# Loads in rows of 8 KB instead of 2, one load tied to another product, and another written-out order for the first block of a fused retention and two-layer feed-forward kernel

## The chip, the cores and the metric

The kernel runs on one core of one Trainium2 chip. The metric is device time in microseconds (us) of one execution, lower is better. Times before the change are a median of 3 runs.

## The reference

Retention (attention with a decaying mask and no softmax) over 4 sequences of 576 positions with 8 heads of 64, then two feed-forward layers over all 2304 tokens, 512 wide inside and 2048 wide in the middle. Everything is float32.

```
scores = scale * q @ k.T                      # per batch and head
ret    = scores * D,  D[i, j] = gamma_h ** (i - j) for i >= j, else 0
x      = (ret @ v) as tokens x 512
x      = leaky(x @ w_in)  @ w_out             # leaky(h) = max(0.01 h, h), weights moe
out    = (h * cos(h)) @ w_out2, h = x @ w_in2 # weights moe2
```

## The kernel before

Every float32 product of the two layers is made of three float32r products: each operand is split into a high part and the low rest, and low*high, high*low and high*high are added up in PSUM. Retention uses plain float32 products of 64 by 64.

Tokens go in 18 chunks of 128 (chunk i) and in 5 blocks (512, 512, 512, 384, 384 tokens). Block 0 is chunks 0 to 3. The middle of 2048 is 16 groups of 128 (f = 0 to 15). A weight group comes from HBM as one tile `raw` of 1 MB (128 partitions of 8 KB) that holds w_in and w_out of that group; the kernel must undo an encoding of the 64-bit words on ScalarE and VectorE and split the result before TensorE can use it. Group 0 and group 15 come as two halves, a (w_in) and b (w_out).

What runs until the end of block 0 is an order written out by hand, the string `FIRST`; each word is a step, and on each engine the instructions stand in the order of the words. The words, with i a chunk and f a group:

- `chI` loads a chunk's q, k, k, v (1 MB, SyncE's queue; chunk 0 in two loads, q and k first); `sqI`, `svI` scale q (VectorE, L249) and v (VectorE L261, or eight small operations on ScalarE, L256).
- `sI` scores (TensorE, L297), `mI` their mask (VectorE, L318), `vI` scores times values (L335), `gI` growth, k times v (L359), `stI.0`, `stI.1` the running state (VectorE, L381 and L383), `rI.0`, `rI` the products with the state (L398), `tkI` copies the result to `xr` (ScalarE, L437). `VI` does v and r of chunk I and g and s of chunk I + 1 in one go.
- `rawF` loads a weight group (L468; halves L473), `absF` and `loF` are ScalarE's part of decoding it (L486, L490), `csF` (two operations, L494 and L496), `orF` (L503) and `addF` (L510) VectorE's; `hiF` is the high part (ScalarE, L519), `lowF` the low rest (VectorE, L522).
- `xhP`, `xlP` split block 0's input (ScalarE L534, VectorE L538; four parts). `HF.P` is the first product of group F (12 products of 512 columns, L550), `lkF`, `ghF`, `glF` leaky and the split of its result (ScalarE L575, L580, VectorE L585), `OF` the second product (12 products, L564).
- `~N` is N times 128 columns of products with a tile of zeros, whose result nobody reads (L456). Of the four such words in the list before all four emit products, 3 + 4 + 5 + 13.

After the list a planner orders blocks 1 to 4, the second layer (products L1197 and L1369) and the conversion of its weights; it works from fixed durations and is the same for any list. The second layer's weights come in pieces of 256 KB, loaded by `convert` (L1052).

All loads are issued by SyncE in the list's order. A wait of one load holds back all loads behind it. Two kinds of such waits are put in by hand with `in_turn`: `raw1` and `raw0b` wait for the scores of chunk 1, and `ch4`, `raw2`, `raw3` wait for the last growth product issued before them (chunk 3's).

The host lays the arrays out. Before, qkv is kept as [chunk][4][128][512], so that one partition's part of a chunk is four pieces of 2 KB, and w as [layer][group][4][128][256 words], also pieces of 2 KB; the loads gather them with a rearranged view.

Of the kernel before, what the change touches and what calls it, by code (L numbers as in the profile page):

```python
# [50 lines left out]


FIRST = """
ch0 sq0 s0 sv0 m0 raw0a abs0a cs0a or0a ~3 v0 g0 st0.0 st0.1 ~4 r0.0 ch1 sq1 s1 r0 lo0a add0a ch2 m1 sq2 sv1
hi0a low0a v1 g1 s2 st1.0 st1.1 r1.0 sv2 m2 v2 r1 ch3 sq3 sv3 raw0b raw1 tk0 g2 st2.0 st2.1 s3 m3 abs0b tk1
cs0b or0b lo0b add0b r2.0 r2 v3 g3 st3.0 st3.1 ~5 r3.0 r3 abs1 cs1 or1 lo1 hi0b low0b add1 tk2 tk3 xh0 xl0 xh1
xl1 ch4 sq4 xh2 xl2 xh3 xl3 hi1 low1 raw2 raw3 abs2 cs2 ~13 H0.0 H0.1 H0.2 H0.3 H1.0 H1.1 H1.2 H1.3 lk0 gh0
gl0 lo2 abs3 or2 add2 lk1 gh1 O0 gl1 O1 cs3 hi2 low2 H2.0 H2.1 H2.2 H2.3 sv4 V3 raw4 lo3 or3 add3 abs4 cs4 hi3
low3 raw5 raw7 raw6 raw8 ch5 raw9 raw15a or4 lk2 gh2 gl2 lo4 add4 abs5 cs5 H3.0 H3.1 H3.2 H3.3 O2 hi4 lk3 low4
H4.0 H4.1 H4.2 H4.3 gh3 gl3 O3 lo5 or5 add5 abs6 cs6 hi5 lk4 gh4 low5 H5.0 H5.1 H5.2 H5.3 gl4 O4 lo7 lo6 abs7  # L60
or6 add6 cs7 hi6 low6 lk5 gh5 gl5 or7 add7 H6.0 H6.1 H6.2 H6.3 O5 abs8 cs8 hi7 lk6 low7 H7.0 H7.1 H7.2 gh6 gl6
st4.0 or8 lo8 add8 st4.1 raw10 lo10 sq5 raw11 H7.3 lk7 gh7 gl7 m4 O6 O7 hi8 low8 H8.0 H8.1 abs9 abs10 lo9 sv5
cs9 or9 add9 raw12 cs10 hi9 low9 H8.2 H8.3 V4 ch6 or10 lk8 gh8 st5.0 gl8 st5.1 add10 abs11 cs11 H9.0 H9.1 H9.2
H9.3 lk9 gh9 gl9 O8 O9 or11 tk4 hi10 low10 H10.0 H10.1 H10.2 H10.3 raw15b raw13 lo11 add11 raw14 sv6 sq6 m5 V5
ch7 abs12 hi11 lk10 gh10 cs12 low11 gl10 or12 lo12 add12 lo13 abs13 H11.0 H11.1 H11.2 H11.3 lk11 gh11 hi12 sv7
lo14 cs13 gl11 st6.0 m6 st6.1 sq7 O10 O11 tk5 low12 H12.0 or13 add13 hi13 H12.1 H12.2 H12.3 lk12 gh12 abs14
low13 abs15a gl12 V6 st7.0 st7.1 cs14 or14 H13.0 H13.1 H13.2 H13.3 add14 lk13 gh13 gl13 O12 O13 cs15a hi14
low14 or15a abs15b tk6 lo15b cs15b ch8 H14.0 H14.1 H14.2 H14.3 sq8 sv8 lo15a m7 add15a hi15a low15a V7 st8.0
lk14 gh14 gl14 st8.1 tk7 H15.0 H15.1 H15.2 H15.3 O14 lk15 or15b add15b gh15 gl15 hi15b low15b O15 m8 ch9 sq9
sv9  # L70
"""


# [1468 lines left out]
```

## Time and profile before

| | |
|---|---|
| median of 3 runs | 834.29 us (833.98 to 834.76) |
| the profiled execution | 833.8 us, of which its span 831.7 us |
| TensorE (PE) busy | 810.5 us, 97% of the span |
| VectorE (DVE) busy | 647.2 us, 78% |
| ScalarE (ACT) busy | 543.8 us, 65% |
| mean granted TensorE clock | 0.994 of full speed |
| DMA | 203.78 MB, mean 245 GB/s |

The span runs from the first to the last instruction; 2.1 us of the execution lie around it. Busy time of PE counts a product until its modelled end, so a busy PE is not PE at its peak. "PEld" is PE's load of the stationary operand, which overlaps its products. All times below are us from the span's start.

### The profile page before, as it was taken

How to read it: one execution, taken by the hardware profiler on the slowest of the kernel's cores; microseconds unless marked ns; L12 is line 12 of the kernel's file. 1: busy time of each engine (PE TensorE's matmuls, PEld its weight loads, DVE VectorE, ACT ScalarE, POOL GpSimd, SP SyncE). 2: the span in 40 equal slices, each digit the busy share in tenths (PEclk: the TensorE clock that was granted, in tenths of full speed). 3: DMA queues.
4: the chain of work that ended last, by engine and by line, in shares of the span. 5: the costliest groups of instructions: out<-in, count | busy, mean ns of one | idle time of the engine just before them, and what ended most of it. 6: DMA issues, size and time to landing. Idle time of an engine off the chain costs nothing.

```text
span 831.7 us, 16073 instructions
## 1 busy us (share of the span) xinstructions
PE 810.5 (97%) x6134; PEld 742.4 (89%) x6134; DVE 647.2 (78%) x1148; ACT 543.8 (65%) x1041; POOL 5.8 (1%) x8
## 2 busy tenths in 40 slices
PE   6999999999999999999999999999999999999996
PEld 4678887888888889999999989989999999999986
DVE  5899987888887868678731297898896888977994
ACT  4788866555555546457432598876878876688761
POOL 0000011000000000000000000000000000000000
PEclk9999999999999999999999999999999999999999
DMA  8774626887777787767688599797866587565632
GB/s 320 271 263 152 229 54 203 267 251 231 266 252 251 244 264 243 250 208 229 216 279 353 209 325 347 239 382 273 290 241 247 218 336 271 169 262 193 250 143 110
DMA packets 101308, 203.78 MB, mean 245 GB/s; under 512 B 9072, under 2 KB 54896, under 8 KB 96112
## 3 DMA queue, kind: packets, MB, share of 16 engines
q1 hardware_dynamic: 101088, 202.41, 69.6%
q8 instruction: 48, 0.79, 0.4%
q10 hardware_dynamic: 144, 0.35, 0.2%
q14 instruction: 28, 0.23, 0.1%
HBM read 147.42 MB, written 55.31 MB: 244 GB/s over the span
## 4 chain that ended last, share of the span: by engine, by line
PE 81%; DVE 8%; DMA 4%; issue 3%; ACT 3%; SPq 0%; DVEq 0%; POOLq 0%; ACTq 0%
PE psum L564 20%; PE psum L550 20%; PE psum L1369 19%; PE psum L1197 19%; DMA ch<-in_qkv 1%; DMA raw<-in_w 1%; PE psum L335 1%; DVE w L522 1%; PE psum L359 1%; DMA ws<-ws 1%; PE psum L398 1%; DVE t L510 1%; DVE t L503 1%; DVE g L1268 1%; PE psum L297 1%
## 5 line engine op out<-in xcount | busy, mean ns | idle before, releaser
L550 PE MATMUL psum<-x_sb,w 128*128 128x512 f32 (+1 forms) x960 | 212.1, 370 | 0.8 <-DVE x_sb L538 0.6
L564 PE MATMUL psum<-g,w 128*128 128x512 f32 (+1 forms) x960 | 211.6, 370 | 0.1
L550 PEld LDWEIGHTS psum<-x_sb,w 128*128 128x128 f32 x960 | 174.7, 188 | 26.1 <-DVE x_sb L538 1.3
L564 PEld LDWEIGHTS psum<-g,w 128*128 128x128 f32 x960 | 174.3, 188 | 24.9 <-DVE g L585 1.6
L1197 PE MATMUL psum<-x,ws 128*128 128x384 f32 x576 | 112.2, 335 | 2.5 <-DMA ws<-ws 1.4
L1197 PEld LDWEIGHTS psum<-x,ws 128*128 128x128 f32 x576 | 100.7, 188 | 3.8 <-DMA ws<-ws 1.7
L1369 PE MATMUL psum<-g,wp 128*128 128x384 f32 x432 | 85.1, 340 | 5.0 <-ACT g L1272 2.8
L851 DVE TENSOR_TENSOR g<-graw,g 128x512 fp32r<-128x512 f32 (+1 forms) x64 | 39.9, 623 | 60.0 <-ACT g L848 59.4
L1197 PE MATMUL psum<-x,wa 128*128 128x384 f32 x432 | 85.2, 335 | 0.0
L1369 PEld LDWEIGHTS psum<-g,wp 128*128 128x128 f32 x432 | 76.3, 190 | 7.2 <-ACT g L1272 3.5
L1369 PE MATMUL psum<-g,wq 128*128 128x384 f32 x432 | 82.3, 334 | 0.1
L1197 PEld LDWEIGHTS psum<-x,wa 128*128 128x128 f32 x432 | 75.8, 188 | 0.2 <-DVE h L1227 0.2
L1369 PEld LDWEIGHTS psum<-g,wq 128*128 128x128 f32 x432 | 75.5, 188 | 0.4 <-DVE acc L1406 0.4
L848 ACT CAST g<-graw 128x512 fp32r<-128x512 f32 (+1 forms) x64 | 36.3, 567 | 52.6 <-PE psum L564 52.4
L844 ACT ACTIVATE graw<-psum 128x512 f32<-128x512 f32 (+1 forms) x64 | 34.6, 541 | 52.5 <-PE psum L550 52.4
L1406 DVE TENSOR_TENSOR acc<-psum,acc 128x384 f32<-128x384 f32 x90 | 49.7, 554 | 18.4 <-PE psum L1369 18.1
L1255 DVE SCALAR_TENSOR_TENSOR h<-r,h 128x768 f32<-128x768 f32 x48 | 45.7, 952 | 15.2 <-ACT r L1252 15.1
L1268 DVE TENSOR_TENSOR g<-tq,g 128x768 fp32r<-128x768 f32 x48 | 45.6, 953 | 6.6 <-ACT g L1272 6.0
L1246 DVE SCALAR_TENSOR_TENSOR r<-r,h 128x768 f32<-128x768 int32 x48 | 45.5, 952 | 1.8 <-ACT r L1241 1.6
L1251 ACT ACTIVATE r<-r 128x768 f32<-128x768 f32 x48 | 40.6, 847 | 8.7 <-DVE r L1246 8.6
L1241 ACT CAST r<-h 128x768 int32<-128x768 f32 x48 | 40.1, 836 | 8.2 <-DVE h L1227 7.9
L1272 ACT CAST g<-tq 128x768 fp32r<-128x768 f32 x48 | 40.1, 838 | 6.0 <-DVE tq L1289 4.2
(115 smaller groups left out, 1055.4 us busy)
## 6 DMA issues: line engine op xcount, KB each, us to landing
ws<-ws SPq DMA_DIRECT2D x20, 1024.0 KB, 5.3
wp<-wp SPq DMA_DIRECT2D x20, 1024.0 KB, 6.7
ch<-in_qkv SPq DMA_DIRECT2D x17, 1024.0 KB, 6.6
x<-xq SPq DMA_DIRECT2D x21, 768.0 KB, 9.2
wa<-wa SPq DMA_DIRECT2D x20, 768.0 KB, 6.0
wq<-wq SPq DMA_DIRECT2D x20, 768.0 KB, 6.3
raw<-in_w SPq DMA_DIRECT2D x14, 1024.0 KB, 10.0
mraw<-in_w SPq DMA_DIRECT2D x32, 256.0 KB, 3.6
```

The source lines that it names most:

```text
L550: nc.tensor.matmul(hp, wt[:, i, cols], x_t[lj, k][:, j, :n], start=(k == 0 and a == 0), stop=(k == KK - 1 and a == 2),)
L564: nc.tensor.matmul(psum[:, BANK_O + m, :n], wt[:, i, cols], gt[:, j, :n], start=(f == 0 and a == 0), stop=(f == NF - 1 and a == 2),)
L851: nc.vector.tensor_tensor(out=g.ap[:, 1, :n], in0=y.ap[:, :n], in1=g.ap[:, 0, :n].bitcast(F32), op=ALU.subtract)
L1197: nc.tensor.matmul(bank[BANKS[m]].rearrange("p (q t) -> p q t", t=Q), a[:, hl, i, j * P : (j + 1) * P], x[:, :, v, j, :], start=m in (1, 5 ...
L1241: "ACT", 885, lambda: nc.scalar.copy(rb.ap.bitcast(I32), pair()),
L1246: nc.vector.scalar_tensor_tensor(out=rb.ap, in0=rb.ap.bitcast(I32), scalar=-1.0, in1=pair(), op0=ALU.mult, op1=ALU.add)
L1251: t = add("ACT", 885, lambda: nc.scalar.activation(rb.ap, rb.ap, AF.Sin, scale=PI), [t], due)
L1255: nc.vector.scalar_tensor_tensor(out=pair(), in0=rb.ap, scalar=0.5, in1=pair(), op0=ALU.subtract, op1=ALU.mult)
L1268: nc.vector.tensor_tensor(out=gb.ap[:, :, 1], in0=src(), in1=gb.ap[:, :, 0].bitcast(F32), op=ALU.subtract)
L1272: h_ = add("ACT", 885 if n == 2 else 515, lambda: nc.scalar.copy(gb.ap[:, :, 0], src()), [*needs, opened["all"]], due, 0, gb.old)
L1369: nc.tensor.matmul(to, wt[:, hl, i, t * P : (t + 1) * P], gt[:, fi, v, :], start=m in (1, 5) and h == 0 and x == 0, stop=h == 1 and x == 2 ...
L1406: x = add("DVE", 560, lambda: nc.vector.tensor_tensor(out=kept(), in0=to, in1=kept(), op=ALU.add), [got], due - SOON / 2)
```

## The change

Four things. The host stores qkv and w so that each partition's part of a chunk or of a weight group is one piece of 8 KB (4 KB for a half, or for each half of chunk 0), and the loads take it in one piece. The second layer's loads of 256 KB still take 2 KB a partition, now 8 KB apart in HBM. `raw1` waits for the scores of chunk 2 instead of chunk 1, and `raw0b` waits for no product. `FIRST` is another list, in which the zero products are 1 + 2 + 12 units of 128 columns instead of 3 + 4 + 5 + 13.

```
 FIRST = """
-ch0 sq0 s0 sv0 m0 raw0a abs0a cs0a or0a ~3 v0 g0 st0.0 st0.1 ~4 r0.0 ch1 sq1 s1 r0 lo0a add0a ch2 m1 sq2 sv1
...
+raw0a abs0a cs0a or0a lo0a add0a ch0 sq0 sv0 s0 m0 ch1 hi0a sv1 ch2 sq1 ~1 v0 g0 s1 sv2 st0.0 st0.1 r0.0 r0
...
         if i == 0:
-            nc.sync.dma_start(ch[:, :2], qkv[i, :2].rearrange("x p d -> p x d"))
-            nc.sync.dma_start(ch[:, 2:], qkv[i, 2:].rearrange("x p d -> p x d"))
+            nc.sync.dma_start(ch[:, :2], qkv[i, :, :2])
+            nc.sync.dma_start(ch[:, 2:], qkv[i, :, 2:])
         else:
-            got = nc.sync.dma_start(ch, qkv[i].rearrange("x p d -> p x d"))
+            got = nc.sync.dma_start(ch, qkv[i])
...
-        return nc.sync.dma_start(raw.rearrange("p (c t) -> p c t", c=4), w[0, f].rearrange("c p t -> p c t"))
+        return nc.sync.dma_start(raw, w[0, f])
...
-        return nc.sync.dma_start(
-            raw.rearrange("p (c t) -> p c t", c=2), w[l, f, 2 * s : 2 * s + 2].rearrange("c p t -> p c t")
-        )
+        return nc.sync.dma_start(raw, w[l, f, :, s * DM : (s + 1) * DM])
...
-            if n == 1 or n == 0 and half:
-                in_turn(got, last_of["scores", 1])
+            if n == 1:
+                in_turn(got, last_of["scores", 2])
...
-                nc.sync.dma_start(rb.ap.bitcast(I64), w[1, f, c])
+                nc.sync.dma_start(rb.ap.bitcast(I64), w[1, f, :, c * 2 * P : (c + 1) * 2 * P])
```

Line numbers of the changed kernel are 2 lower from L473 on (L522 is now L520, and so on).

TensorE at the start, before: after three warming products, scores of chunk 0, and then a zero product ahead of v0 and another ahead of the first state product.

```order
L450 MATMUL psum<-zero 128x512 x3
L297 MATMUL psum<-ch 64x64 x16
L456 MATMUL psum<-tabs_sb,still 128x384
L335 MATMUL psum<-p_sb,ch 64x64 x16
L359 MATMUL psum<-ch 64x64 x16
L456 MATMUL psum<-tabs_sb,still 128x512
L398 MATMUL psum<-ch,st 64x64 x4
L297 MATMUL psum<-ch 64x64 x16
L398 MATMUL psum<-ch,st 64x64 x4
L335 MATMUL psum<-p_sb,ch 64x64 x16
L359 MATMUL psum<-ch 64x64 x16
L297 MATMUL psum<-ch 64x64 x16
```

The same place of the changed kernel, up to the first product with chunk 1's state.

```order
L450 MATMUL psum<-zero 128x512 x3
L297 MATMUL psum<-ch 64x64 x16
L456 MATMUL psum<-tabs_sb,still 128x128
L335 MATMUL psum<-p_sb,ch 64x64 x16
L359 MATMUL psum<-ch 64x64 x16
L297 MATMUL psum<-ch 64x64 x16
L398 MATMUL psum<-ch,st 64x64 x8
L297 MATMUL psum<-ch 64x64 x16
L335 MATMUL psum<-p_sb,ch 64x64 x16
L359 MATMUL psum<-ch 64x64 x16
L335 MATMUL psum<-p_sb,ch 64x64 x16
L359 MATMUL psum<-ch 64x64 x16
```

The scores of chunk 2 (the third L297) now stand ahead of v1 and g1, one zero product is shorter and one is gone.

VectorE's first work before: q and v of chunk 0 are scaled first, the decoding of raw0a (t_156) comes behind the mask.

```order
L249 TENSOR_TENSOR ch<-ch,tabs_sb 128x512
L261 TENSOR_TENSOR ch<-ch,tabs_sb 128x512
L318 TENSOR_TENSOR p_sb<-psum,tabs_sb 128x512
L494 TENSOR_SCALAR t_156<-t_156 128x512
L496 TENSOR_SCALAR t_156<-t_156 128x512
L503 SCALAR_TENSOR_TENSOR t_156<-raw,t_156 128x512
```

VectorE's first work in the changed kernel.

```order
L492 TENSOR_SCALAR t_133<-t_133 128x512
L494 TENSOR_SCALAR t_133<-t_133 128x512
L501 SCALAR_TENSOR_TENSOR t_133<-raw,t_133 128x512
L508 ISA t_133<-raw,t_133 128x1024
L249 TENSOR_TENSOR ch<-ch,tabs_sb 128x512
L261 TENSOR_TENSOR ch<-ch,tabs_sb 128x512
L318 TENSOR_TENSOR p_sb<-psum,tabs_sb 128x512
```

All four decoding steps of raw0a now stand ahead of chunk 0's scaling.

SyncE's loads before: chunk 0 in two, raw0a, chunks 1 to 3, raw0b, raw1, then (behind chunk 3's growth) chunk 4, raw2 and more.

```order
L238 DMA ch<-in_qkv 128x2x512
L239 DMA ch<-in_qkv 128x2x512
L473 DMA raw<-in_w 128x2x256
L241 DMA ch<-in_qkv 128x4x512 x3
L473 DMA raw<-in_w 128x2x256
L468 DMA raw<-in_w 128x4x256
L241 DMA ch<-in_qkv 128x4x512
L468 DMA raw<-in_w 128x4x256 x7
```

SyncE's loads in the changed kernel; the five at L468 are raw1, raw3, raw2, raw4 and raw6, of which raw3 is the first behind chunk 3's growth.

```order
L473 DMA raw<-in_w 128x512
L238 DMA ch<-in_qkv 128x1024
L239 DMA ch<-in_qkv 128x1024
L241 DMA ch<-in_qkv 128x2048 x3
L473 DMA raw<-in_w 128x512
L468 DMA raw<-in_w 128x1024 x5
L241 DMA ch<-in_qkv 128x2048
```

raw0a moved ahead of chunk 0, and chunk 4 moved from the first place behind chunk 3's growth to the fifth.

## Rows read from the trace of the kernel before

**Rows 1.** The page: busy time by engine, and the queue of instruction fetches.

```profile
PE 810.5 (97%) x6134; PEld 742.4 (89%) x6134; DVE 647.2 (78%) x1148; ACT 543.8 (65%) x1041; POOL 5.8 (1%) x8
...
q8 instruction: 48, 0.79, 0.4%
```

**Rows 2.** Windows: stretch, length, busy per engine, granted clock, DMA share, GB/s.

```profile
20.00:25.00 5.00, 3.10 (x126) 2.96 (x126) 2.56 (x6) 3.47 (x6) 0.00 (x0) 0.79 0.04 14
25.00:30.00 5.00, 4.84 (x52) 2.69 (x46) 4.83 (x8) 3.54 (x11) 0.00 (x0) 0.87 0.68 218
...
50.00:60.00 10.00, 10.00 (x45) 8.14 (x44) 9.80 (x13) 7.61 (x10) 0.00 (x0) 1.00 0.61 223
...
90.00:100.00 10.00, 10.00 (x164) 8.29 (x163) 9.26 (x12) 9.63 (x18) 0.00 (x0) 1.00 0.74 236
```

**Rows 3.** Timeline of TensorE, 0 to 49 us: start, us, instruction, idle before.

```profile
15.73 0.69 PE L297 MATMUL psum<-ch 64*64 64x64 f32 x32 [0.62 <-DVE ch L249]
...
19.07 0.28 PE L297 MATMUL psum<-ch 64*64 64x64 f32 x2
21.74 0.63 PE L297 MATMUL psum<-ch 64*64 64x64 f32 x27 [2.40 <-issue]
...
24.15 1.09 PE L359 MATMUL psum<-ch 64*64 64x64 f32 x32
...
31.38 1.66 PE L550 MATMUL psum<-x_sb,w 128*128 128x512 f32 x6 [0.33 <-DVE x_sb L538]
...
43.92 2.97 PE L550 MATMUL psum<-x_sb,w 128*128 128x512 f32 x12
```

**Rows 4.** Windows from the start: (x) counts recorded products (PE) and weight loads (PEld).

```profile
0.00:9.00 9.00, 7.03 (x72) 3.21 (x76) 2.61 (x5) 2.00 (x3) 0.20 (x4) 1.00 0.80 282
...
0.00:14.70 14.70, 10.87 (x204) 5.92 (x208) 6.81 (x13) 5.27 (x13) 0.20 (x4) 1.00 0.90 322
...
0.00:19.40 19.40, 13.89 (x348) 8.41 (x348) 10.80 (x21) 8.66 (x26) 0.20 (x4) 1.00 0.94 339
```

**Rows 5.** DMA queues in 12.6:13.9, 19.1:20.4 and 22.7:23.7: count, MB, share of 16 engines.

```profile
q8 instruction: 1, 0.02, 5.4%
...
q8 instruction: 1, 0.02, 5.3%
...
q8 instruction: 1, 0.02, 5.5%
```

**Rows 6.** Windows in which only loads run: pieces of 2 KB, then of 6 and 8.

```profile
15.00:19.00 4.00, 2.37 (x130) 2.03 (x127) 3.87 (x7) 3.01 (x12) 0.00 (x0) 1.00 1.04 386
...
442.00:450.00 8.00, 8.00 (x48) 8.00 (x48) 1.12 (x2) 2.01 (x4) 0.00 (x0) 1.00 1.02 426
```

**Rows 7.** Timeline, 0 to 50 us: first users of loads, and the load behind chunk 3's growth.

```profile
5.84 0.69 DVE L249 TENSOR_TENSOR ch<-ch,tabs_sb 128x512 f32<-128x512 f32 x1 [4.31 <-DMA ch<-in_qkv]
...
7.15 0.69 DVE L261 TENSOR_TENSOR ch<-ch,tabs_sb 128x512 f32<-128x512 f32 x1 [0.61 <-DMA ch<-in_qkv]
...
8.48 0.70 ACT L486 ACTIVATE t<-raw 128x512 f32<-128x512 f32 x1 [5.80 <-DMA raw<-in_w]
...
14.98 0.69 DVE L249 TENSOR_TENSOR ch<-ch,tabs_sb 128x512 f32<-128x512 f32 x1 [1.19 <-DMA ch<-in_qkv]
...
25.32 0.37 SPq L241 DMA_DIRECT2D ch<-in_qkv  x1
...
34.68 1.13 ACT L486 ACTIVATE t<-raw 128x1024 f32<-128x1024 f32 x1 [2.40 <-DMA raw<-in_w]
```

**Rows 8.** The same timeline: VectorE's cs0b, add0b, st3 and low2.

```profile
23.10 0.42 DVE L494 TENSOR_SCALAR t<-t 128x512 f32<-128x512 f32 x1
...
24.84 0.69 DVE L510 CUSTOM_DVE_ANT_0 t<-raw,t 128x1024 uint16<-128x1024 uint16 x1
...
25.45 0.95 DVE L383 TENSOR_TENSOR st<-psum,st 128x256 f32<-128x256 f32 x2
...
42.22 1.22 DVE L522 TENSOR_TENSOR w<-t,w 128x1024 fp32r<-128x1024 f32 x1
```

More of the change, by code (lines that the diff above doesn't have):

```diff
@@ L53 @@
 FIRST = """
-ch0 sq0 s0 sv0 m0 raw0a abs0a cs0a or0a ~3 v0 g0 st0.0 st0.1 ~4 r0.0 ch1 sq1 s1 r0 lo0a add0a ch2 m1 sq2 sv1
[L55 to L58, printed above, removed]
@@ L64 @@
[L64 to L68, printed above, removed]
@@ L69 @@
-lk14 gh14 gl14 st8.1 tk7 H15.0 H15.1 H15.2 H15.3 O14 lk15 or15b add15b gh15 gl15 hi15b low15b O15 m8 ch9 sq9
-sv9
+raw0a abs0a cs0a or0a lo0a add0a ch0 sq0 sv0 s0 m0 ch1 hi0a sv1 ch2 sq1 ~1 v0 g0 s1 sv2 st0.0 st0.1 r0.0 r0
+tk0 ch3 low0a sq2 m1 s2 m2 v1 g1 st1.0 v2 g2 sq3 s3 sv3 st1.1 r1.0 r1 raw0b raw1 m3 v3 g3 raw3 raw2 raw4 abs0b
+cs0b st2.0 st2.1 lo0b or0b add0b r2.0 r2 st3.0 st3.1 tk1 abs1 lo1 cs1 or1 add1 tk2 ~2 r3.0 r3 tk3 xh0 xl0 xh1
+xl1 xh2 xl2 hi0b raw6 ch4 raw5 ch5 raw8 raw15a xh3 hi1 raw7 raw9 raw15b low0b abs2 xl3 ~12 H0.0 H0.1 H0.2 H0.3
@@ new lines @@
+low1 H1.0 H1.1 H1.2 H1.3 lk0 gh0 lo2 abs3 cs2 gl0 or2 add2 O0 lk1 gh1 gl1 O1 cs3 hi2 sq4 low2 lo3 or3 H2.0
+H2.1 H2.2 H2.3 sv4 abs4 add3 cs4 V3 hi3 lk2 low3 H3.0 H3.1 H3.2 H3.3 gh2 gl2 O2 or4 lo4 add4 abs5 cs5 hi4 lk3
+low4 H4.0 H4.1 H4.2 H4.3 or5 gh3 gl3 O3 lo5 add5 abs6 cs6 hi5 low5 or6 lk4 lo6 gh4 gl4 add6 abs7 cs7 lo7 hi6
+H5.0 H5.1 H5.2 H5.3 O4 lk5 gh5 raw10 low6 or7 gl5 abs8 cs8 sq5 add7 sv5 H6.0 H6.1 H6.2 H6.3 O5 lk6 gh6 gl6 O6
+hi7 st4.0 or8 low7 lo8 add8 hi8 abs9 H7.0 H7.1 H7.2 H7.3 st4.1 m4 V4 lk7 gh7 lo9 low8 raw11 lo11 abs10 cs9 or9
@@ new lines @@
+add9 hi9 raw12 H8.0 H8.1 H8.2 H8.3 gl7 O7 ch6 cs10 lk8 gh8 low9 abs11 lo10 H9.0 H9.1 H9.2 H9.3 gl8 O8 st5.0
+st5.1 tk4 lk9 m5 or10 add10 gh9 gl9 sq6 O9 hi10 low10 H10.0 H10.1 H10.2 H10.3 cs11 or11 add11 lo12 abs12 sv6
+cs12 raw13 hi11 low11 raw14 V5 ch7 m6 lk10 lo13 gh10 or12 gl10 st6.0 add12 st6.1 H11.0 H11.1 H11.2 H11.3 lk11
+gh11 gl11 hi12 low12 O10 O11 abs13 H12.0 H12.1 H12.2 H12.3 sv7 cs13 or13 add13 sq7 tk5 V6 abs14 hi13 low13
+lk12 gh12 gl12 cs14 or14 lo14 add14 H13.0 H13.1 H13.2 H13.3 lk13 gh13 gl13 O12 O13 hi14 low14 H14.0 H14.1
@@ L71 @@
+abs15a st7.0 st7.1 m7 H14.2 H14.3 ch8 abs15b tk6 cs15a lo15a or15a add15a hi15a low15a sv8 sq8 V7 lk14 cs15b
+or15b gh14 gl14 lo15b add15b m8 hi15b low15b H15.0 H15.1 H15.2 H15.3 lk15 gh15 gl15 O14 O15 st8.0 st8.1 tk7
+ch9 sq9 sv9
 """
```

9 lines of the change are left out of this document (2 added, 7 removed).

## The prediction

> **What bounds the kernel now.** I read the page first, then the windows, then TensorE's timeline of the first 50 us. PE is busy 97% of the span [rows 1]. From 50 us on a window shows it busy all the time, and VectorE nearly so in block 0: 9.80 and 9.26 of 10 us [rows 2]. A list for the beginning can thus change little but when that state begins: what is won before H2 moves everything behind it, which the planner orders as before.
>
> Three things hold the beginning. (1) PE stands still for 2.40 us at 19.3, two products into the scores of chunk 3, and the row names no releaser, only "issue" [rows 3]. The rows on instruction fetches explain it. PE's 12268 recorded instructions (6134 products, 6134 weight loads) over 48 fetches [rows 1] make 256 a fetch. PE stops with 348 + 348 = 696 recorded [rows 4]; borders 256 apart then lie at 184, 440 and 696. The first is passed at about 9.2 (148 recorded at 9.0) and the second at about 15 (412 at 14.7) [rows 4]. Fetches start at about 12.7, 19.2 and 22.75 [rows 5]: 3.5 and 4.2 us after those borders while loads run, and 1.0 us after PE goes on at 21.74 [rows 3], when DMA is idle (14 GB/s) [rows 2]. Each holds one DMA engine for about 1.1 us (5.4% of 16 engines in 1.3 us) [rows 5]. The second ends at 20.3, PE goes on 1.4 us later. So code fetched beside saturated loads comes 6 to 7 us after its border, and PE has one block of 256 to live on meanwhile. (2) After the stop the clock is granted at 0.79 and 0.87 in the mean of two windows [rows 2], a stretch at 1.2 GHz. (3) Chunk 3's growth ends at 25.24 (24.15 + 1.09) [rows 3]; call that G. Only then SyncE issues the next loads, at 25.32, and raw2, the second of them, is first used at 34.68, G + 9.4, after ScalarE waited 2.40 us for it [rows 7]. From there VectorE works through to low2 at 42.22 = G + 17.0 [rows 8], and H2 starts at 43.92 [rows 3].
>
> **The change, part by part.** *Rows of 8 KB.* Pieces of 2 KB move at 386 GB/s, pieces of 6 and 8 KB at 426 [rows 6]: 1 MB takes 2.5 us instead of 2.7. The 3.5 MB up to chunk 2 are the same loads in both; at 426 they gain 0.9 us, and I take 0.7, since raw0a and chunk 0 come in pieces of 4 KB. Chunk 2 also loses the first fetch in front of it, 1.1 us (below). I put its landing at 13.2 instead of 14.98 [rows 7]. Then chunk 3, raw0b and raw1 follow without a gap, 6.2 us and one fetch of 1.1: the queue is empty at about 20.5. On this the Trainium skill speaks against the change: "DMA: Bandwidth & Descriptors", section "Where 436 GB/s comes from", holds that between HBM and SBUF the HBM side binds at about 358 GB/s. The rows stand above that with both sizes; by that rule nothing of the gain would come.
>
> The second layer's 256 KB loads, 2 KB out of 8, have no like in the trace. They feed the second layer alone, four blocks later; at no loss and at double their time the price is nothing, and a gain there is worth nothing either.
>
> *raw0a first.* It lands where chunk 0's first half did, 5.84, and VectorE's sq0 now stands behind its decoding: 0.70 on ScalarE [rows 7], then 0.43 twice and 0.69 twice [rows 8], 2.9 us. sv0 no longer waits 0.61 for its load [rows 7]. PE's work on chunk 0 comes 2.3 later, so border 184, again in g0, is passed at 11.5 instead of 9.2.
>
> *The order of the products.* With 64 recorded instructions to each group of 16 plain float32 products, the new row is: warming 12, s0 76, zeros 80, v0 144, g0 208, s1 272, r0 304, s2 368, v1 432, g1 496, v2 560, g2 624, s3 688, r1 752. Border 440 now falls at the start of g1, 696 into r1. Chunk 2 at 13.2 lets s2 run at 13.9 and g1 at 15.1, only 3.6 us after border 184. The fetch asked for at 11.5 starts at 15.0 (3.5 later, as before), ends at 16.1 and feeds PE at 17.5. So there is a stop of 2.4 us in g1 that the old order did not have: it reached 440 later, and there s2 waited for data until 15.73 [rows 3]. The next fetch is asked for at 17.5. Its wait lies between 1.0 (idle) and the emptying of the queue at 20.5, so it starts between 18.5 and 20.5; I take 19.5, since by then most engines are empty. PE goes on 2.5 later, at 22.0 (21.0 to 23.0); about 20 it stood at r1, so this stop is some 2 us, in the place of the old one. Behind it stand 92 products up to the end of g3, against 126 before, which took 3.5 us from 21.74 at the low clock: 2.6 us. With two stops of over 2 us I expect the low clock again. G becomes 24.6, 0.6 earlier. Bounds: 21.0 + 1.5 at full clock = 22.5 (2.7 earlier), 23.0 + 2.7 = 25.7 (0.5 later).
>
> *From G to low2.* VectorE has the same operations between st3 and low2 in both orders; sq4 moves from ahead of the wait for raw2 to behind it, 0.6 us more there, and two loads of 0.25 less each put raw2 0.5 earlier. raw2 is second behind G in both. This cancels: low2 at G + 17.0 = 41.6. The new G can hold it, since SyncE's next loads still wait for g3. What is late next is raw2, as now.
>
> *Zero products and the wait of raw1.* The zero products lie where PE waits for VectorE; the last row ahead of H0 is one unit shorter and ends about when the split input does, so 0. raw1 behind s2 is asked for at 14.5, when 4 us of loads are still queued: 0. If that queue were empty, raw1 would land some 2 us late, still ahead of its decoding, which stands behind st3.
>
> *The rest of block 0.* From low2 on, VectorE and PE are both nearly full and the groups come in nearly the same order. In the new list cs15b (two operations of 0.43) stands behind low15a instead of ahead: 0.9 us at the last group if VectorE binds, nothing if PE does. I take 0.5.
>
> **Sum.** 0.6 + 0.5 = 1.1 us. Against the profiled execution, 833.8 us (2.1 of it outside the span), that is 832.7; the median lies 0.5 higher, so 833.2.
>
> **Rivals.** *B, no stop.* If the fetches keep up, VectorE runs through from chunk 2's landing: 1.8 earlier landing, 0.6 for low0a, which is done ahead of it, and the 2.4 idle us of 20:25 [rows 2] vanish. That is 4.8, with the last term 5.3: 829.0. For it: everything else in the beginning is ready. Against it: two fetches under load took 6 us and more, and the new row reaches the border sooner after the last one. *C, a short stop.* The second fetch starts at 18.5 and the clock stays up: G at 22.5, 3.2 in all, 831.1. For it: the queue drains while it waits. *D, slower.* One mechanism: the second fetch comes only behind raw1, and raw1 lands at 22.2 or later, because the early rows move no faster and the first fetch's engine carries it last. PE then goes on at 24.7, G is 27.3 or more, 2.1 late, less 0.5: 835.9 and up. It decides from a queue empty after 22.3. By the skill's 358 GB/s (page and section above) such a queue would be the rule; the 386 of the trace [rows 6] already contradict it. *E, the rows are no faster and the stops only change place:* 834.3.
>
> **How the numbers follow.** About 0.2% (1.7 us) is what a measurement of this kernel can tell from no change. The forecast's case, stops moved and G a little earlier: 0.55, own range 831.1 to 834.8; of it 0.14 faster by over 0.2%, 0.38 within, 0.03 slower. B 0.17 and C 0.15, both faster. D 0.09, slower. E 0.04, within. Faster 0.46, within 0.42, slower 0.12. The range goes from 828.8 (just under B) to 835.6, which leaves out most of D.
>
> **What would show it.** In the new profile: DMA at some 420 GB/s in 5 to 15; VectorE's first scaling at about 8.8; a row of PE with idle time "issue" of about 2.4 in L359 (g1) near 15 to 17.5 and one in L398 (r1) up to about 22, with 440 and 696 recorded; fetches at about 15 and 19.5; the first load behind g3 at 24.6; H0 near 30, low2 at 41.6; a lower clock in 18 to 26. Without the "issue" rows B is right, and low2 stands at about 37.5. If the stops are there and G is after 27, D is. If low2 moves but the end does not, the rest of block 0 was mis-sized.

## The result: 0.5% slower, outside the predicted range

| | kernel before | changed kernel |
|---|---|---|
| median | 833.31 us (831.45 to 835.91, 20 runs) | 837.69 us (834.55 to 841.26, 20 runs) |
| ratio, 95% interval | | 1.0051 [1.0039, 1.0063] |
| profiled execution, span | 833.8, 831.7 us | 837.48, 835.3 us |

Predicted were 833.2 us and 828.8 to 835.6. The change costs 4.4 us, and the profiled executions differ by about as much (3.6 us of span), so the trace may be asked where. The page's first row:

```profile
PE 809.0 (97%) x6128; PEld 742.0 (89%) x6128; DVE 646.3 (77%) x1148; ACT 544.2 (65%) x1041; POOL 5.3 (1%) x8
```

PE is busy 1.5 us less than in [rows 1] in a span 3.6 longer: what was lost is idle time of PE. The windows, columns as in [rows 2]:

```profile
5.00:10.00 5.00, 1.17 (x3) 0.31 (x1) 2.84 (x6) 1.80 (x3) 0.00 (x0) 0.87 1.03 423
10.00:15.00 5.00, 4.70 (x130) 4.10 (x130) 2.76 (x6) 3.18 (x14) 0.00 (x0) 0.50 1.01 423
15.00:20.00 5.00, 3.16 (x109) 2.67 (x112) 2.47 (x4) 2.83 (x10) 0.00 (x0) 0.84 0.68 238
20.00:25.00 5.00, 4.18 (x183) 3.91 (x181) 3.73 (x8) 0.73 (x3) 0.00 (x0) 0.77 0.26 102
...
80.00:90.00 10.00, 9.83 (x44) 7.80 (x42) 7.59 (x11) 8.14 (x17) 0.00 (x0) 1.00 0.27 98
90.00:100.00 10.00, 8.85 (x157) 7.24 (x157) 9.86 (x13) 8.28 (x15) 0.00 (x0) 1.00 0.54 177
```

Loads run at 423 GB/s now, against 386 in [rows 6]. But PE works 1.17 of the five us up to 10, its clock is granted at 0.50 in the next five (1.2 GHz), and in 90:100, where it had 10.00 [rows 2], it has 8.85. TensorE's timeline shows the places (start, us, instruction, idle before):

```profile
10.05 1.14 PE L297 MATMUL psum<-ch 64*64 64x64 f32 x32 [3.88 <-DVE ch L249]
...
12.91 1.08 PE L359 MATMUL psum<-ch 64*64 64x64 f32 x32
...
17.41 0.31 PE L359 MATMUL psum<-ch 64*64 64x64 f32 x5
19.39 1.01 PE L359 MATMUL psum<-ch 64*64 64x64 f32 x26 [1.67 <-issue]
...
22.57 0.33 PE L398 MATMUL psum<-ch,st 64*64 64x64 f32 x3
23.58 1.04 PE L398 MATMUL psum<-ch,st 64*64 64x64 f32 x28 [0.68 <-issue]
...
24.91 0.65 PE L359 MATMUL psum<-ch 64*64 64x64 f32 x32
...
32.55 1.65 PE L548 MATMUL psum<-x_sb,w 128*128 128x512 f32 x6 [0.72 <-DVE x_sb L536]
...
44.33 2.95 PE L548 MATMUL psum<-x_sb,w 128*128 128x512 f32 x12
...
91.15 2.14 PE L562 MATMUL psum<-g,w 128*128 128x512 f32 x8 [1.32 <-DVE g L583]
```

The two stops for code stand where the prediction put them, in g1 (L359) and in r1 (L398). They end at 19.39 and 23.58, not at 17.5 and 22.0. Chunk 3's growth ends at 25.56, 0.3 later than in [rows 3], H0 starts 1.2 later, H2 0.4 later. VectorE's timeline has the third place, and the end of the beginning, low2 (42.22 in [rows 8]):

```profile
9.31 0.69 DVE L249 TENSOR_TENSOR ch<-ch,tabs_sb 128x512 f32<-128x512 f32 x1
...
43.00 1.22 DVE L520 TENSOR_TENSOR w<-t,w 128x1024 fp32r<-128x1024 f32 x1
...
87.41 0.69 DVE L318 TENSOR_TENSOR p_sb<-psum,tabs_sb 128x512 f32<-128x512 f32 x1 [2.16 <-ACT xr L437]
```

The last row is m5. It stands in the new list right behind tk4 and lk9, and VectorE idles 2.16 us until ScalarE has done tk4 (xr). Behind m5 wait the decoding of group 10 and gl9 (L583), and O9 waits for gl9: the 1.32 us of PE above.

From here on "lag" is the start of one and the same product in a run's trace less its start in the trace of the kernel before. The changed kernel's lag is +0.4 us at H2, +2.2 at O9, +2.2 still at 200 us, +4.7 at 350, and 3.6 at the end of the span. Between 200 and 350 ScalarE waits longer for the second layer's pieces (26.6 us in 12 waits, 15.3 in 10 in the kernel before). The waits on the tile mraw in 200:352, changed kernel (us, times), then the page's DMA issues with the median us to landing (3.6 for both names before):

```profile
  DMA mraw<-in_w: 26.6, 12
...
mraw<-in_w SPq DMA_DIRECT2D x32, 256.0 KB, 4.3
more<-in_w SPq DMA_DIRECT2D x32, 256.0 KB, 4.2
```

### The profile page after: what moved, and what is told of

The parts are those of the page before. It is cut to its first block, busy times and chain, and to the rows that moved or that the text cites. A ratio compares the mean times of both kernels' runs of the same rounds, so it can differ in the third digit from the quotient of the medians.

```text
span 835.3 us, 16067 instructions
## 1 busy us (share of the span) xinstructions
PE 809.0 (97%) x6128; PEld 742.0 (89%) x6128; DVE 646.3 (77%) x1148; ACT 544.2 (65%) x1041; POOL 5.3 (1%) x8
## 4 chain that ended last, share of the span: by engine, by line
PE 74%; DVE 11%; DMA 6%; issue 4%; ACT 4%; SPq 0%; DVEq 0%; ACTq 0%; POOLq 0%
PE psum L1367 19%; PE psum L1195 18%; PE psum L562 17%; PE psum L548 16%; DMA more<-in_w 2%; DMA mraw<-in_w 1%; PE psum L335 1%; PE psum L359 1%; DMA ws<-ws 1%; PE psum L398 1%; PE psum L297 1%; DVE t L501 1%; DVE g L1266 1%; DMA mt<-y 1%; DVE acc L1404 1%
## 5 line engine op out<-in xcount | busy, mean ns | idle before, releaser
L1404 DVE TENSOR_TENSOR acc<-psum,acc 128x384 f32<-128x384 f32 x90 | 49.7, 555 | 17.1 <-PE psum L1367 16.8
```

Of the source, the lines that this page charges most:

```text
L1404: x = add("DVE", 560, lambda: nc.vector.tensor_tensor(out=kept(), in0=to, in1=kept(), op=ALU.add), [got], due - SOON / 2)
```

## The experiments

Each was timed against the kernel before, in 6 to 12 executions. Three theories stood at first. **Theory 1**: the list costs about half (start and m5) and the strided loads of the second layer the other half. **Theory 2**: the list alone. **Theory 3**: the layout alone. All results, with the lags of the profiled execution:

| run | ratio, 95% interval | H0 | H2 | O9 | at 200 | at 350 |
|---|---|---|---|---|---|---|
| changed kernel | 1.0051 [1.0039, 1.0063] | +1.2 | +0.4 | +2.2 | +2.2 | +4.7 |
| e1_list_only | 1.0046 [1.0028, 1.0063] | | | | | |
| e8_list_again | 1.0059 [1.0036, 1.0081] | +2.2 | +1.2 | +3.6 | +4.7 | +5.0 |
| e2_layout_only | 1.0034 [1.0017, 1.0051] | +1.1 | +0.3 | +0.2 | +0.3 | +1.0 |
| e5_rows_old_list | 1.0029 [1.0009, 1.0050] | +2.0 | +1.2 | +1.1 | +2.3 | +2.3 |
| e4_w2_strided | 1.0017 [0.9995, 1.0039] | -0.2 | -0.7 | -0.7 | -0.7 | -0.5 |
| e3_w2_whole | 1.0035 [1.0017, 1.0054] | +1.2 | +0.4 | +2.2 | +3.4 | +3.4 |
| e6_w2_whole_m5_later | 1.0018 [1.0003, 1.0033] | +1.7 | +1.0 | +1.3 | +1.6 | +1.6 |
| e12_m5_later | 1.0023 [1.0002, 1.0045] | +1.6 | +0.8 | +1.1 | +2.3 | +2.3 |
| e7_chunk0_first | 1.0049 [1.0032, 1.0067] | +1.4 | +0.7 | +2.5 | +2.4 | +4.3 |
| e13_zeros16 | 1.0045 [1.0027, 1.0062] | +0.7 | -0.1 | +1.7 | +2.2 | +2.4 |
| e9_rows_hold | 0.9998 [0.9980, 1.0017] | +2.2 | +0.9 | +0.8 | +2.2 | +2.2 |
| e10_before_hold | 0.9985 [0.9966, 1.0004] | -1.1 | -1.5 | -1.5 | -1.4 | -1.4 |
| e15_hold_weight_rows | 0.9992 [0.9973, 1.0011] | +0.4 | -0.9 | -0.9 | -0.9 | -0.7 |
| e11_new_list_hold | 1.0055 [1.0034, 1.0075] | +5.2 | +4.2 | +4.7 | +4.9 | +4.9 |
| e14_new_list_hold2 | 1.0060 [1.0040, 1.0080] | +3.6 | +2.7 | +3.1 | +5.0 | +5.0 |

Executions of one kernel spread with a standard deviation of 1.0 to 2.7 us, so a lag is that of one execution and the ratio that of many. A difference of two ratios is uncertain by about 0.0022 to 0.0028.

### The list or the layout (e1, e2, e8)

e1 has the layouts of before with the new list and its waits; e2 the new layouts with the old ones. e8 is e1 once more: the one profiled execution of e1 took 1002 us, against 834.46 to 838.48 in its other eight, and its trace is not read.

> The old layouts (pieces of 2 KB everywhere), but the new list and the new waits of raw1 and raw0b. In the two traces the changed kernel is 0.8 us late at low2, 2.2 us late from O9 on (VectorE stands 2.16 us at m5, which waits for ScalarE's copies tk4) and 4.4 us late after block 2, where ScalarE waits for the second layer's weight pieces. Theory 1 (two causes, the list about half and the second layer's loads the other half): 2 to 3 us slower than before, that is some 835.8, and at the end of block 0 about as late as the changed kernel. Theory 2 (the list alone): 4 us slower. Theory 3 (the layout alone): no change from before.

> The new layouts (8 KB for chunks and first-layer weights, second-layer weights as 2 KB out of 8), but the old list and the old waits. Theory 1: the beginning gains a little (chunk 2 earlier by 0.7 us or so, the stop of 2.4 us in the scores of chunk 3 stays), blocks 1 to 4 lose some 2 us on the second layer's loads: 1 to 2 us slower than before. Theory 2: no slower, up to 1 us faster. Theory 3: 4 us slower.

> The list and its waits alone, on the rows of 2 KB of the kernel before, once more, for a profile that is not disturbed. Theory 1: the lag behind the kernel before is about 1 to 2 us at H0 (chunk 2 lands later than with rows of 8 KB), rises by 1.4 at O9, then stays flat through blocks 1 to 4 (whole stretches of 256 KB); ratio 1.003 to 1.005. Theory 2 (the list alone does it, by its start alone): the lag is 3 us or more at low2 and does not rise at O9.

Each half alone costs: the list 1.0046 and 1.0059, the layout 1.0034. So theories 2 and 3 fall. The parts add up to more than the whole, so that neither is a share of the 4.4 us. Theory 1 falls in its detail: the layout alone, without the new list, should have cost only the strided loads' part in blocks 1 to 4 and 1 to 2 us; it cost 2.8, and its H0 was already late (+1.1, of which 0.3 is left at H2).

### The second layer's loads (e3, e4)

e3 is the changed kernel with whole stretches of 256 KB for the second layer (the host keeps that layer as before), e4 the kernel before with strided ones.

```
-                nc.sync.dma_start(rb.ap.bitcast(I64), w[1, f, :, c * 2 * P : (c + 1) * 2 * P])
+                two = w[1, f].rearrange("p t -> (p t)").rearrange("(c p t) -> c p t", c=4, p=P)
+                nc.sync.dma_start(rb.ap.bitcast(I64), two[c])
```

> The changed kernel with one thing undone: the second layer's weights are kept in HBM so that each load of 256 KB is one whole stretch again. Theory 1: 2 us faster than the changed kernel (some 835.5), with the lag against before constant from O9 to the end of block 4. Theory 2: as the changed kernel, 837.6. Theory 3: back to 833.3.

> The kernel before with one thing done: the second layer's weights are kept in HBM with 8 KB a partition, so that each load of 256 KB takes 2 KB out of every 8. Theory 1: some 2 us slower than before (835.5), all of it lost in blocks 1 to 4, and a longer time to landing for these pieces (4.2 us instead of 3.6). Theory 2: no change. Theory 3: up to 4 us slower.

The same rows for e3 (waits on mraw in 200:352, then DMA issues):

```profile
  DMA mraw<-in_w: 12.8, 6
...
mraw<-in_w SPq DMA_DIRECT2D x32, 256.0 KB, 3.5
```

The landing and the waits go back with the stretches (3.6 us and 15.3 us in the kernel before), and the lag no longer grows from 200 to 350. Over all traces: the six with strided loads (changed kernel, e2, e4, e7, e12, e13) grow by 0.0 to 2.5 us there, mean 0.9; the nine with whole stretches by 0.3 at most, mean 0.1. The four timed pairs that differ in this alone (changed kernel and e3, e12 and e6, e4 and before, e2 and e5) differ by 0.0016, 0.0005, 0.0017 and 0.0005, mean 0.9 us. No pair alone is certain, and the mean is uncertain by about 1.0 us. The estimate is thus 0.9 us, half of what theory 1 had, and the sign rests on times and traces together.

### m5 (e6, e12)

```
-... tk4 lk9 m5 or10 add10 gh9 gl9 sq6 O9 ...
+... tk4 lk9 or10 add10 gh9 gl9 sq6 m5 O9 ...
```

e12 is the changed kernel with this alone, e6 with whole stretches too.

> The changed kernel with the second layer's weights in whole stretches of 256 KB, and m5 moved behind gl9 in the list. Theory 1: VectorE's stop of 2.16 us at 87.4 (m5 behind tk4) goes, O9 starts 1.3 us earlier, the lag behind the kernel before falls from 2.2 to 0.9 us at O9 and to some 0.5 at O15; the time is 1.4 us under that of the changed kernel with whole stretches alone, ratio 1.0035 less 0.0017 = 1.002. Rival (VectorE is full there, so the wait only moves): O9 is no more than 0.3 us earlier, or O15 keeps its lag of 1.8 us, and the ratio stays at 1.0035.

> The changed kernel with m5 moved behind gl9 and nothing else. Theory 1: O9 is reached 1.3 us earlier, the time is 1.2 to 1.6 us under the changed kernel's, ratio 1.0033 to 1.0037; what stays above the run that also has whole 256 KB stretches (1.0018) is the price of the strided loads, 1.3 to 1.6 us, and shows as a lag that grows between 200 and 350 us. Rival (the strided loads cost nothing in the timed runs): the same ratio as with the whole stretches, 1.002 or below.

VectorE and TensorE of e12, the same place:

```profile
89.25 0.69 DVE L583 TENSOR_TENSOR g<-graw,g 128x512 fp32r<-128x512 f32 x1 [1.07 <-ACT g L578]
89.86 0.68 DVE L249 TENSOR_TENSOR ch<-ch,tabs_sb 128x512 f32<-128x512 f32 x1
90.46 0.68 DVE L318 TENSOR_TENSOR p_sb<-psum,tabs_sb 128x512 f32<-128x512 f32 x1
```

```profile
87.40 5.62 PE L562 MATMUL psum<-g,w 128*128 128x512 f32 x24
```

gl9 starts at 89.25 instead of 90.41, m5 waits no longer, and O8 and O9 are 24 products without a gap. From H2 to O9 the lag grows by 1.75 to 1.8 us in the four traces of the new list and rows with m5 in its place (changed kernel, e3, e7, e13) and by 0.3 in e6 and e12. By O15 some of it has gone again: from H2 to O15 the lag grows by 1.4 to 1.5 us in the four and by 0.4 to 0.5 in e6 and e12, so 1.0 us is left. In time: 1.0051 to 1.0023 and 1.0035 to 1.0018, 2.3 and 1.4 us, the mean uncertain by about 1.4. One word of the list thus costs a third to a half of the loss. e6's rival (the wait only moves) falls.

e12 missed what was said of its strided loads. The price of these was to show as a ratio of 1.0033 to 1.0037 and as a lag that grows between 200 and 350 us; the ratio is 1.0023, next to its rival's 1.002, and the lag does not grow (+2.3 at both), though the pieces land in 4.2 us here too.

### The start: order and clock (e7, e13)

e7 puts chunk 0 ahead of raw0a again; e13 gives PE 16 units of zero products while it waits.

```
-raw0a abs0a cs0a or0a lo0a add0a ch0 sq0 sv0 s0 m0 ch1 ...
+ch0 sq0 sv0 s0 m0 raw0a abs0a cs0a or0a lo0a add0a ch1 ...
...
-raw0a abs0a cs0a or0a lo0a add0a ch0 sq0 sv0 s0 m0 ch1 ...
+raw0a abs0a cs0a or0a lo0a add0a ch0 sq0 sv0 ~16 s0 m0 ch1 ...
```

> The changed kernel with the one part of its list undone that puts raw0a and its decoding ahead of chunk 0. Theory 1 (the start loses because VectorE's first scaling stands behind the decoding: PE idles 3.88 us before s0 and its clock falls to 0.50 in 10:15): s0 starts near 7, the clock stays up in 10:15, the growth of chunk 3 ends 0.8 us or more earlier than 25.56, H0 at 31.7 instead of 32.55, low2 at 42.2, ratio 1.003 instead of 1.005. Rival (the two stops for code set the start, wherever the scaling stands): the stops are again in g1 and r1, the second ends at 23.5 or later, low2 stays at 43.0 within 0.3 us and the ratio at 1.005.

> The changed kernel with 16 more units of zero products ahead of chunk 0's scores, so that PE is busy while it waits for VectorE's first scaling. Clock theory (the start loses because the granted clock falls to 0.50 in 10:15 after 3.88 us without work): the groups of chunk 0 and the scores of chunk 1 take 0.69 instead of 1.1 us, chunk 3's growth ends 0.5 us or more earlier than 25.56, H0 at 32.0 or earlier, ratio 1.0035 to 1.0045. Rival (VectorE and the fetches set the start): the clock is up, but the growth of chunk 3 and H0 stay within 0.3 us and the ratio at 1.005.

TensorE of e7:

```profile
17.60 1.01 PE L359 MATMUL psum<-ch 64*64 64x64 f32 x26 [0.24 <-issue]
...
23.16 1.06 PE L398 MATMUL psum<-ch,st 64*64 64x64 f32 x28 [2.00 <-issue]
```

The scores of chunk 0 start at 7.50 instead of 10.05, and nothing is won: the first stop shrinks to 0.24, the second grows to 2.00. The rival is right in the main: ratio 1.0049, low2 at 43.30; only its second stop ends at 23.16, not at 23.5 or later. In e13 the clock stays at 1.00 in 10:15 (0.50 in the changed kernel):

```profile
10.00:15.00 5.00, 3.72 (x151) 3.00 (x150) 3.97 (x8) 3.23 (x14) 0.00 (x0) 1.00 1.01 423
```

Chunk 3's growth ends 0.9 earlier and H0 starts 0.5 earlier, as the clock theory said, and the time falls by 0.0006, the least of what it said and less than the intervals tell. By the traces the low clock costs about half a us at H0, not the 4.4; the times do not show it.

### Why rows of 8 KB cost at the start (e5, e9, e10, e15)

e5 has the old list, 8 KB rows for chunks and first layer, whole stretches for the second.

> The old list and its waits, 8 KB rows for the chunks and the first layer's weights, the second layer's weights kept as whole stretches of 256 KB. Theory 1 (the list's start and m5 cost about 0.8 and 1.4 us, the strided 256 KB loads about 1 to 2 us, the 8 KB rows themselves nothing): ratio 0.999 to 1.001, within 1 us of the kernel before, no waits of ScalarE for mraw beyond those of before. Theory 3 (the 8 KB rows themselves cost time, for instance because the fetches of code come later behind larger transfers): as slow as the layout alone, 1.0034 or 2.8 us, with the first products H0 about 1 us late.

It is as slow as the layout alone: theory 3's part is real. TensorE shows the stop of [rows 3] in the scores of chunk 3 again, 3.65 us instead of 2.40, though chunk 2 lands earlier. A stop of 0.76 us at the border before it, in the scores of chunk 2, is new. VectorE shows the first scaling late:

```profile
19.35 0.28 PE L297 MATMUL psum<-ch 64*64 64x64 f32 x2
23.28 1.02 PE L297 MATMUL psum<-ch 64*64 64x64 f32 x27 [3.65 <-issue]
```

```profile
6.68 0.69 DVE L249 TENSOR_TENSOR ch<-ch,tabs_sb 128x512 f32<-128x512 f32 x1 [5.14 <-DMA tabs_sb<-in_tabs]
```

Hence **theory F**: the second fetch of PE's code stands behind raw0b and raw1, which are issued early, and comes sooner when they wait. e9 is e5 and e10 the kernel before, both with one word changed; e15 is e10 with 8 KB rows for the first layer's weights alone.

```
             if n == 1 or n == 0 and half:
-                in_turn(got, last_of["scores", 1])
+                in_turn(got, last_of["scores", 2])
```

> The kernel of the run on the rows alone (old list, 8 KB rows, second layer's weights in whole stretches), but raw0b and raw1 wait for the scores of chunk 2 instead of chunk 1. Theory F (the rows cost time because the second fetch of PE's code stands behind loads that leave no gap): the second fetch starts near 18 instead of 21.1, the stop inside the scores of chunk 3 falls from 3.65 to under 1.5 us, chunk 3's growth ends at 24.5 instead of 27.4, and the time falls by 1.5 to 2.5 us, ratio 0.999 to 1.001. Rival (the rows lose it at the first load, chunk 0's first half landing at 6.5 instead of 5.7, or later than the start): the stop goes, but ratio stays above 1.002. Rival 2 (the fetch comes no earlier when loads are held): the stop stays over 3 us.

> The kernel before with one wait changed: raw0b and raw1 wait for the scores of chunk 2 instead of chunk 1. Theory F: the second fetch starts near 17.5 instead of 19.2, PE's stop of 2.40 us inside the scores of chunk 3 falls under 1 us, chunk 3's growth ends at 23.5 instead of 25.2, H0 1.5 us earlier, ratio 0.9975 to 0.999. Rival (raw1 now lands late enough to be waited for, or PE's stop only moves): H0 and the time as before, ratio 0.9995 to 1.001.

> The kernel before with raw0b and raw1 waiting for the scores of chunk 2, and rows of 8 KB for the first layer's weights only; chunks keep their 2 KB pieces, the second layer its whole stretches. If the rows of the chunks cost at the first load (4 KB pieces of chunk 0 land 0.7 to 0.9 us later): chunk 0's scores start at 6.9 as in the kernel before, not at 7.5, and the time is that of the run on 2 KB rows with the same waits, 0.9985, or below by up to 0.5 us. Rival (the first landing is hidden by what follows): the time is that of the run with all rows of 8 KB and the same waits, 0.9998.

TensorE of e9, then of e10 (scores of chunk 3, its growth, the next zero product, H0):

```profile
19.68 0.28 PE L297 MATMUL psum<-ch 64*64 64x64 f32 x2
20.33 0.69 PE L297 MATMUL psum<-ch 64*64 64x64 f32 x30 [0.38 <-issue]
...
27.63 0.49 PE L456 MATMUL psum<-tabs_sb,still 128*128 128x128 f32 x2 [3.58 <-issue]
```

```profile
20.21 0.97 PE L297 MATMUL psum<-ch 64*64 64x64 f32 x32
...
22.86 0.65 PE L359 MATMUL psum<-ch 64*64 64x64 f32 x32
...
25.37 0.49 PE L456 MATMUL psum<-tabs_sb,still 128*128 128x128 f32 x2 [0.80 <-issue]
...
30.23 1.65 PE L550 MATMUL psum<-x_sb,w 128*128 128x512 f32 x6 [0.37 <-DVE x_sb L538]
```

The stop falls from 3.65 to 0.38 in e9 and from 2.40 to nothing in e10. A third one, one border later, appears behind the loads that were held, 3.58 us in e9 and 0.80 in e10. With the wait e9 is back at 0.9998 from e5's 1.0029, so the time at which raw0b and raw1 are issued decides over what the rows of 8 KB cost in e5, 2.4 us. That it does so through the fetch is not shown by e9's trace: its third stop eats what the second gives back, and H0 starts as late as in e5 (+2.2 and +2.0). That execution took 836.89 us, the longest of its twelve (median 833.30). e10 goes 1.1 us earlier at H0; its ratio, 0.9985, lies where theory F put it, but the interval reaches 1.0004, so that it beats the kernel before is likely and not shown. e15 starts its scores at 6.87 as expected (6.59 in the kernel before), and its ratio cannot tell 0.9985 from 0.9998: the first landing's price stays open.

### The same wait in the new list (e11, e14)

Both are e6 with waits added; e14 has the first of these edits, e11 the other two.

```
-            if n == 1:
+            if n == 1 or n == 0 and half:
                 in_turn(got, last_of["scores", 2])
...
+            if i == 3:
+                in_turn(got, last_of["scores", 1])
...
-            if n == 1:
-                in_turn(got, last_of["scores", 2])
+            if n == 1 or n == 0 and half:
+                in_turn(got, last_of["scores", 3])
```

> The changed kernel with whole 256 KB stretches and m5 moved, and in addition chunk 3's load waiting for the scores of chunk 1, raw0b and raw1 for those of chunk 3. Theory F: the first fetch starts near 14 instead of 17 and the first stop (1.2 to 1.7 us, in the growth of chunk 1) goes, the second falls under 1 us or goes; chunk 3's growth ends at 24.3 instead of 25.6 to 26.1; ratio 0.999 to 1.001 against 1.0018 without the waits. Rival (the start is set by VectorE and the low clock, not by the fetches): the stops go, but chunk 3's growth and H0 move by under 0.4 us and the ratio stays at 1.002.

> The changed kernel with whole 256 KB stretches and m5 moved (ratio 1.0018), and raw0b waiting for the scores of chunk 2, as raw1 already does; chunk 3 waits for nothing. Theory F: the first fetch is no earlier than 16.5, since chunk 3 still lies ahead of it, but the queue is empty behind chunk 3, so that the second fetch comes before PE needs it: the second stop (0.6 us) goes, the first stays; ratio 1.000 to 1.0015. Rival (the held raw0b is late for its decoding, as with the longer wait): VectorE waits for it ahead of st2, chunk 3's growth or H0 are later than 26.1 and 33.1, ratio 1.003 or more.

TensorE of e11, ScalarE of e11, TensorE of e14:

```profile
23.18 1.10 PE L361 MATMUL psum<-ch 64*64 64x64 f32 x32
28.06 0.71 PE L400 MATMUL psum<-ch,st 64*64 64x64 f32 x16 [3.79 <-DVE st L385]
```

```profile
25.56 0.66 ACT L486 ACTIVATE t<-raw 128x512 f32<-128x512 f32 x1 [8.04 <-DMA raw<-in_w]
```

```profile
17.17 0.91 PE L359 MATMUL psum<-ch 64*64 64x64 f32 x31
...
20.12 0.33 PE L398 MATMUL psum<-ch,st 64*64 64x64 f32 x4 [0.24 <-DVE st L383]
24.52 1.53 PE L398 MATMUL psum<-ch,st 64*64 64x64 f32 x28 [4.07 <-issue]
```

e11 has no stop left, as theory F said, and is slower all the same: raw0b lands at 25.5, ScalarE stands 8.04 us for it, VectorE's cs0b stands behind ScalarE, st2 behind cs0b, and PE behind st2. In e14 I had the two stops the wrong way round: the first is gone (its fetch comes at 15.0, not after 16.5), the second is 4.07 us, because raw0b and raw1 are issued at 16.75 and 17.1, just before PE comes to the next border. e11 and e14 are slower than e6 by 3.1 and 3.5 us: in the new list no run shows a gain from holding these loads. The queue of instruction fetches in 22.1:23.1 of e14, then in 13.8:14.9 and 19.2:20.3 of e11:

```profile
q8 instruction: 1, 0.02, 5.6%
```

```profile
q8 instruction: 1, 0.02, 5.2%
...
q8 instruction: 1, 0.02, 5.5%
```

Put together, when PE reaches the group with the border and when the fetch starts. In e5 and e9 PE stands for code inside s2 (0.76 and 1.03 us), and the time is that at which it goes on:

| run, border | PE there | loads issued and not landed | fetch starts | later by |
|---|---|---|---|---|
| e11, first | g0 12.9 | chunk 2 | 13.9 | 1.0 |
| e14, first | g0 12.8 | chunks 2, 3 | 15.0 | 2.2 |
| changed kernel, first | g0 12.9 | chunks 2, 3, raw0b | 17.0 | 4.1 |
| e9, second | s2 16.9 | rest of chunk 3 | 18.1 | 1.1 |
| e11, second | g1 17.4 | chunk 3 | 19.2 | 1.8 |
| e5, second | s2 16.6 | rest of chunk 3, raw0b, raw1 | 21.1 | 4.5 |
| e14, second | g1 17.2 | raw0b, raw1 | 22.2 | 5.0 |

In these rows a fetch starts when the loads issued ahead of it have been moved, or all but the last of them: 5.0 of 5.0 MB in the changed kernel, 5.8 of 6.0 in e14's second. But a fetch does not wait for everything that is queued. The loads' queue up to the first fetch, in the changed kernel (0:17.04) and in the kernel before (0:12.69; count, share, and MB of a million bytes, where the text's MB have 1024 KB):

```profile
q1 hardware_dynamic: 1006, 5.24, 76.6%
```

```profile
q1 hardware_dynamic: 1826, 3.61, 76.9%
```

5.24 is all up to raw0b. Of the 4.72 issued in the kernel before only 3.61 had been moved, and most of chunk 3 was still to come. Ten traces have such a first fetch. Between PE's passing the border, by the count of recorded instructions, and the start of the fetch 1.2 to 1.3 MB were moved where the chunks come in pieces of 2 KB (kernel before, e4, e8, e10, e15), and 1.3 to 2.1 MB with rows of 8 KB (e2, e5, e7, e9, e13). So the delay grows with what is queued up to such an amount, and larger rows can make it longer.

The Trainium skill, "DMA: Bandwidth & Descriptors", section "Queues, rings and completion order", says that each DMA engine goes round the queues packet by packet, a packet being 9 to 17 descriptors typically. If a piece is a descriptor, one packet on each of 16 engines is, as an estimate from the page's figure, 1.1 to 2.1 MB with pieces of 8 KB and 0.3 to 0.5 MB with pieces of 2 KB. The first agrees with what the fetches waited for, the second does not (1.2 to 1.3); whether packets are longer there, no run shows.

## Why the prediction was wrong, point by point

- **8 KB rows faster: right in rate, short in what it gives.** 423 GB/s against 386. The Trainium skill's 358 GB/s ("DMA: Bandwidth & Descriptors", section "Where 436 GB/s comes from") does not bind here: both rates stand above it. But chunk 2 landed at 13.9, not 13.2, and its first scaling, behind other work of VectorE, came at 15.49.
- **Stops in g1 and r1: right in place, late in time.** Border 184 was to be "passed at 11.5": g0 started at 12.91, since sq0 came at 9.31 (8.8 said) and the groups ran at half clock, which I expected only after 18. The fetch, at 17.0, then followed its border (184 recorded at 13.35) by 3.7 us, about the 3.5 assumed. The second was to start 2.0 us after PE went on, and did (19.39 to 21.34). Both stops are late mostly because the first border is. One reading behind the 3.5 is off: the kernel before passes border 440 at 15.73, when the scores of chunk 2 start, not at about 15, so that its second fetch too comes 3.5 us after its border and not 4.2. "H0 near 30, low2 at 41.6": 32.55 and 43.00, the latter 17.4 behind G and not 17.0. Chunk 3's growth was to come 0.6 earlier and came 0.3 later, still within the bound of 0.5 that the text gave.
- **The rest of block 0, "0.5": wrong step, and the largest.** "The groups come in nearly the same order" passed over one word: m5 right behind tk4. With VectorE at 9.26 of 10 us [rows 2], a wait of 2.16 us there is made good only in part (1.0 us is left at O15). By the times it costs 1.4 to 2.3 us, where a gain of 0.5 stood.
- **The second layer's loads, whose price "is nothing": wrong step, by the estimate.** "Four blocks later" holds for the products, not for the conversion: ScalarE takes these pieces in blocks 1 to 4, stands for them, and the leaky of block products stands behind. About 0.9 us, uncertain by 1.0; 2.5 in the profiled execution, none in e12's.
- **The waits of raw1 and raw0b, "0": wrong as a view of them.** For their own use they land early enough, as the text said (raw1 was issued only at 17.0 into an emptied queue and landed at 21.9). But that raw0b waits for nothing puts it ahead of the first fetch (17.0, against 15.0 in e14), and in the old list the same two loads are ahead of the second. When a load is issued was the largest lever of the start, for better in e9 (2.6 us) and for worse in e14 (3.5 us), and the text had it at nothing. That another time would have made the changed kernel faster is not shown.

The profiled execution is thus accounted for: 0.4 at H2, 1.8 from there to O9, 2.5 from 200 to 350, and 1.1 given back by the end, 3.6 us. Of the timed 4.4 us, start (0.7, the mean lag at H2 of the changed kernel, e3, e6, e7 and e12), m5 (1.4 to 2.3) and strided loads (0.9) make 3.0 to 3.9; the rest is open.

A candidate is the start of block 1: between O9 and 200 us some traces lose another 1.1 to 1.9 us (e3, e5, e8, e9, e12, e14) and the others under 0.5, with either list and either layout. The traces show the place. The first products of block 1 wait for VectorE's split of its input (x_sb), and GpSimd scales a chunk at that time (L249, L261). Kernel before, then e3:

```profile
130.29 1.04 POOL L261 TENSOR_TENSOR ch<-ch,tabs_sb 128x512 f32<-128x512 f32 x1
131.18 2.50 DVE L786 TENSOR_TENSOR x_sb<-xr,x_sb 128x512 fp32r<-128x512 f32 x4
```

```profile
133.01 4.19 DVE L784 TENSOR_TENSOR x_sb<-xr,x_sb 128x512 fp32r<-128x512 f32 x4
...
133.96 1.50 POOL L261 TENSOR_TENSOR ch<-ch,tabs_sb 128x512 f32<-128x512 f32 x1
```

Where GpSimd is done within 0.2 us of the split's start, the four operations take 2.49 to 2.58 us (kernel before, e2, e4, e10, e11, e15); where it goes on for 0.3 to 0.6, 2.68 to 2.94 (e6, e7, changed kernel); where it goes on for 0.7 to 2.5, 3.09 to 4.28 (e3, e5, e8, e9, e12, e13, e14). In the changed kernel's trace this is 0.4 us. That GpSimd's work is the cause is read from these sixteen traces; no run moved it.

Rival D (slower) had the sign, and slower had a chance of 0.12. Its mechanism came in part: the second fetch did start only when raw1's bytes had been moved (21.34). But raw1 landed at 21.9, not at 22.2 or later, and chunk 3's growth ended 0.3 us late, not 2.1. Most of the loss came from steps that D does not have.

## What to carry to other kernels

Where an engine runs through its code faster than it is fetched, loads issued ahead of need are not free: of what is queued when a code border is passed, one to two MB were waited for here, and the time of one load's issue, one word of a wait, was worth more than 10% of load rate: 2.6 us won in the old list, 3.5 lost in the new one. A new order is to be read word by word on the engine that is nearly full: one instruction placed right behind another engine's late one cost more than the whole change of layout was to bring. A load's price is to be looked for where its data are first touched, not where they are multiplied.
